# Second-layer and output weight splits in steps free of other work, with V's upper halves made by ScalarE

## The chip, the cores and the metric

The program runs on one core of a Trainium2 chip. A core has TensorE (PE in the profile, with its weight loads as PEld), VectorE (DVE), ScalarE (ACT), GpSimd (POOL) and SyncE (SP, which here only issues DMAs), and each engine works through its own queue in order. The metric is the device time of one execution in microseconds (us), as the median over the runs; less is better.

## The reference

The inputs are x (1 x 2048 x 640), wqkv (640 x 1920), wo (640 x 640), w1 (640 x 1536), b1, w2 (1536 x 640) and b2. A layer norm of x feeds two branches, and the result is the sum of x and both:

```python
xn = _layernorm(x)
return x + _A_ref(xn, wqkv, wo) + _B_ref(xn, w1, b1, w2, b2)
```

Branch A is attention with 32 heads of 20 columns each: q, k, v from `xn @ wqkv`, softmax of the scaled scores over all 2048 keys, times v, then `@ wo`. Branch B normalises `xn` once more, multiplies by w1, adds b1, applies the tanh form of gelu, multiplies by w2 and adds b2. Everything is float32 outside.

## The kernel before, in words

**Numbers in two halves.** A float32 operand of a product is split into an upper and a lower float16 half, and a product is three TensorE passes over them (upper-upper, upper-lower, lower-upper). Splitting a weight in place costs a scaling (`wtmp`), a cast to the upper half and a subtraction for the lower half. V is kept per block of 128 keys in `vfull`: blocks 0, 1, 4, 5, 8, 9, 12, 13 as an upper and a lower half (`SPLIT[kb]` is 1), the others whole.

**The head** (the first 186 us of the trace) takes x in four chunks of 512 rows: normalise, transpose (`pt`, then `xnt` in two halves: ScalarE casts the upper one, VectorE subtracts), and five pairs of q and k column blocks per chunk (`qk`), whose results leave PSUM through `qk_out` (ScalarE writes the upper half of `qkhl`, VectorE the lower half). `qk_sq` squares them (`sq`; in chunk 0 on ScalarE) for a bound on the scores. The order here is written out by hand, a string of letters for each pair, in which each letter is a step. V's columns of the first 8 heads are made here, and V of the last four key blocks whole.

**The loop** runs over 64 stretches: a pair of heads, one half of the query rows, one 512-column part of it. I call such a stretch an iteration. In it 16 units, one for each key block, each make scores (`s`, two matmuls), their exponentials on ScalarE (`p`, 128 x 1024), for the 8 split blocks a lower half on VectorE (`low`), and the product with V (`o`). ScalarE ends an iteration by moving `o` from PSUM (`ev`). Scores have three PSUM buffers, `p` has seven buffers and `low` four.

**What sets the order.** The table `PLAN` has seven rows for each iteration. `s` is a unit's scores, `lN` unit N's lower half, `v4` the V products of four units, `e` the evacuation, `t` and `r` each one tick, and `m` one slot for other TensorE work. The other TensorE work comes from one generator (`mlp`, then `projection`): for row chunk 0 of branch B the six first-layer products (`pu`), then V's remaining columns of the first twelve key blocks (`values`, product `pz`), then chunks 1 to 7 with the second layer (`py`), then the output projection (`z`). All of these use one PSUM buffer of one bank, `psM`, so that a product begins only when the one before has been read out. In each `m` slot so much of it is taken as a credit of some 1.9 us allows.

**Side work.** Everything that VectorE and ScalarE do for it (gelu, `values_out`, weight splits, stack loads) is a generator that takes one step for each tick. Those in the list `sides` take a step in every tick. Those in the list `patient` take one only if nothing else in that tick named a cost above zero. `values_out` runs its instructions when the last matmul of its `pz` is recorded and names a cost for the next tick. `second_split` splits w2 in 12 pieces, two steps each; `prep_late` loads wo into w1's place and splits it in 5 pieces, three steps each.

Of the kernel before, what the change touches and what calls it, by code (L numbers as in the profile page):

```python
# [13 lines left out]
AF = mybir.ActivationFunctionType  # L14
ALU = mybir.AluOpType
# [3 lines left out]
P = 128  # L19
# [16 lines left out]
RATE = (1.75, 1.95, 1.9)  # L36
PLAN = ('s s t l0 v4 e', 's s t l1 s r m r r l4', 's s l5 v4', 's s r t m', 's s s l8 r v4', 's l9 t l12 s l13 m', 's r s v4')
UNITS = (3, 3, 3, 3, 2, 2)
# [10 lines left out]
def mha_mlp_kernel(tc, x, wqkv, wo, w1, b1, w2, b2, out):  # L49
# [4 lines left out]
    with (  # L54
# [124 lines left out]
        with tc.tile_pool(name="pa", bufs=2) as pa, tc.tile_pool(name="pa1", bufs=1) as pa1, tc.manual_schedule():  # L179
# [181 lines left out]
            def qk_out(c, tt, ps):  # L361
                hl = stp.tile([P, 2, 2, 512], F16, tag="ks", name="qkhl")

                parts = ((0, 2),) if tt != 2 else ((0, 1), (1, 2))
                for i0, i1 in parts:
                    a = qks[:, (2 * tt + i0) // KD : (2 * tt + i0) // KD + 1]
                    nc.scalar.activation(hl[:, 0, i0:i1], ps[:, i0:i1], AF.Copy, scale=a)  # L367
                    nc.vector.scalar_tensor_tensor(hl[:, 1, i0:i1], ps[:, i0:i1], a, hl[:, 0, i0:i1],  # L368
                                                   ALU.mult, ALU.subtract)
                if c + tt > 0:  # L370
                    qk_sq(c, tt, hl)
                for s in range(2):
                    nc.sync.dma_start(
                        qkscr[s, 2 * tt * P : (2 * tt + 2) * P, c * 512 : (c + 1) * 512]
                        .rearrange("(i p) t -> p i t", p=P), hl[:, s])
                return hl
# [243 lines left out]
            for c in range(4):  # L620
                nxt = c + 1 if c < 3 else None
                for tt in range(5):
# [11 lines left out]
                    if c == 0:  # L634
# [5 lines left out]
                        elif tt == 1:  # L640
                            qk_sq(0, 0, hl)
                            pts = []
                    for step in (('', 'qvo', 'ao', 'bo', '4q!y@c#otyxttywz'), ('zos', 'qa6yqoPsbiqs', 'jkso', 'lcsV4o', 'sxoy'), ('ssoa6bzijP', 'yo', 'zs4ossc', 'klozV', 'uozs'), ('so', 'os6', 'oszs', 'ssosPsVfze4', 'o'))[c][tt]:
                        if step == "a":
# [29 lines left out]
                        elif step == "f":  # L674
                            factors_out()
                        elif step == "o":
                            qk_out(c, tt, ps)
                        elif step == "P":
# [25 lines left out]
        with ExitStack() as scope:  # L704
# [359 lines left out]
            def layer1(mc, f, spare=False):  # L1064
# [24 lines left out]
                if f == KF - 2:  # L1089
                    if 0 < mc < NMC - 2:  # L1090
                        load_chunk(mc + 2)
                    if mc + 1 == NMC:
                        sides.append(ahead())
                        sides.append(prep_late(wot, wov, wo.rearrange("(k p) n -> p k n", p=P), KD, 8))

# [8 lines left out]
            def layer2(mc, j, hf):  # L1104
# [5 lines left out]
                for f in range(KF):  # L1110
                    for a, b in PASS:
# [4 lines left out]
                        if n % 2 == 0:  # L1116
                            if n == 36:
                                begin(addup(ps, xbs[t0], t0, hf))
                            yield 0.272

            def second_split():

# [8 lines left out]
            def values_out(kb, ps):  # L1131

                pv_ = ps[:, : D - VC].rearrange("p (h d) -> p h d", d=DH)
                vs = (V16 if SPLIT[kb] else V32)[:, kb, VH:]
                nc.vector.tensor_scalar(vs[:, :, :DH], pv_, 2.0**-14, None, ALU.mult)  # L1135
                if SPLIT[kb]:
                    nc.vector.scalar_tensor_tensor(vs[:, :, VW : VW + DH], pv_, 2.0**-14, vs[:, :, :DH],  # L1137
                                                   ALU.mult, ALU.subtract)
                yield 1.2 if SPLIT[kb] else 0.6

            def values(hv, feats):

                step = (D - VC) / 2400
                for kb in range(NKB - 4):
                    c, j = divmod(kb, MC // P)
                    if kb == 8:
                        yield 1, 0.2
# [5 lines left out]
                        nc.vector.tensor_scalar(fo, pw["v"][0], 2.0**-22, pw["o"][0], ALU.mult, ALU.mult)  # L1153
                        sides.append(second_split())
                        yield 0.2
# [17 lines left out]
            def mlp():  # L1173
# [3 lines left out]
                for mc in range(NMC + 1):  # L1177
# [3 lines left out]
                    for i in range(6):  # L1181
# [7 lines left out]
                        if second and i % 3:  # L1189

                            yield 3 * KF // 2, 4.896
                            yield from second.pop(0)
# [275 lines left out]
```

## Time and profile before

| | |
|---|---|
| median of 3 runs | 1330.71 us (1330.6 to 1332.67) |
| the profiled execution's own time | 1334.18 us |
| its span, first to last instruction | 1332.3 us |
| PE busy in the span | 1317.0 us (99%) |
| ACT busy | 1111.4 us (83%) |
| DVE busy | 1072.6 us (81%) |
| granted TensorE clock | 0.996 of full speed |
| iterations of the loop, `ev` to `ev`, from 256.07 to 306.30 us | 16.97, 15.97 and 17.29 us |
| the next four | 18.51, 18.38, 18.41 and 17.16 us |

The busy time of PE is modelled, and a matmul that starts late behind a wait in its own group can still be counted as busy. So a full row of nines for PE does not say that it ran at its own pace; the length of like iterations does. A ScalarE or VectorE instruction's duration is from its start to its end, and two neighbours may overlap by a little.

### The profile page before, as it was taken

What the parts mean: (1) busy time and instruction counts of PE and PEld (TensorE: products, weight loads), DVE (VectorE), ACT (ScalarE), POOL (GpSimd) and SP (SyncE); (2) the same over time, 40 slices, a digit from 0 to 9 for tenths busy, and PEclk for the clock granted to TensorE, in tenths of its full rate; (3) what the DMA queues carried; (4) which work ended last, traced back from release to release, by engine and by line L of the source; (5) the groups of instructions that cost most, each with busy time, mean ns of one, the idle gap of its engine ahead of it and who ended that gap; (6) DMA issues with size and microseconds to landing.
All of it is one profiled execution on the core that took longest, in us unless ns stands there. A gap on an engine that the chain in (4) does not pass through costs nothing.

```text
span 1332.3 us, 29076 instructions
## 1 busy us (share of the span) xinstructions
PE 1317.0 (99%) x11636; PEld 606.0 (45%) x11636; DVE 1072.6 (81%) x1462; ACT 1111.4 (83%) x1294; POOL 36.3 (3%) x85
## 2 busy tenths in 40 slices
PE   9999999999999999999999999999999999999998
PEld 6455564333344444444444444444444444443466
DVE  6767659868999987889888888988889898988642
ACT  6744459898899999999999999999999999989900
POOL 2000000000000000000000000000000000000000
PEclk8999999999999999999999999999999999999999
DMA  8687631121223321142312033321124232253276
GB/s 286 216 268 211 197 122 35 39 68 42 62 79 102 93 54 32 47 117 69 98 51 64 20 88 117 81 56 58 49 58 118 91 83 73 71 157 98 88 218 188
DMA packets 108166, 135.28 MB, mean 102 GB/s; under 512 B 24308, under 2 KB 74376, under 8 KB 107900
## 3 DMA queue, kind: packets, MB, share of 16 engines
q1 hardware_dynamic: 104588, 125.99, 31.2%
q0 software_dynamic: 2816, 6.90, 2.7%
q8 instruction: 92, 1.51, 0.5%
q10 hardware_dynamic: 624, 0.51, 0.1%
q14 instruction: 46, 0.38, 0.1%
HBM read 86.64 MB, written 43.74 MB: 98 GB/s over the span
## 4 chain that ended last, share of the span: by engine, by line
PE 78%; DVE 13%; DMA 3%; ACT 3%; issue 2%; SPq 1%; ACTq 0%; DVEq 0%
PE o L816 25%; PE s L784 16%; PE pu L1077 10%; PE py L1112 10%; PE qkp L352 8%; DVE low L798 6%; PE z L1255 5%; ACT p L786 2%; PE pz L1161 2%; PE vp L425 1%; DVE w2t L1128 1%; DMA xb<-in_B_b_dram 1%; DVE u L1008 1%; DVE u L1010 1%; PE vp L446 1%
## 5 line engine op out<-in xcount | busy, mean ns | idle before, releaser
L786 ACT ACTIVATE p<-s 128x1024 f32<-128x1024 f32 x1024 | 968.4, 1053 | 68.2 <-PE s L784 66.6
L798 DVE TENSOR_TENSOR low<-p 128x1024 f16<-128x1024 f32 x512 | 605.5, 1219 | 65.8 <-ACT p L786 64.7
L816 PE MATMUL o<-p,vfull 128*32 128x512 bf16 (+1 forms) x4096 | 384.0, 493 | 0.0
L784 PE MATMUL s<-qs,ks 61*128 61x512 f16 x2048 | 302.9, 381 | 2.5 <-ACT p L786 1.7
L784 PEld LDWEIGHTS <-ks 61*128 61x128 f16 x2048 | 74.9, 94 | 231.4 <-issue 212.8
L1077 PE MATMUL pu<-xm,w1t 128*128 128x256 f16 x1440 | 171.4, 273 | 1.4 <-DVE vfull L1135 1.4
L1112 PE MATMUL py<-w2t,hT 128*128 128x320 f16 x1152 | 171.6, 300 | 1.2 <-DVE xb L1039 1.2
L1077 PEld LDWEIGHTS <-w1t 128*128 128x128 f16 x1440 | 134.3, 98 | 45.6 <-issue 31.1
L816 PEld LDWEIGHTS <-vfull 128*32 128x32 f16 x3072 | 61.3, 95 | 186.8 <-issue 186.2
L1112 PEld LDWEIGHTS <-hT 128*128 128x128 f16 x1152 | 105.6, 98 | 71.5 <-issue 34.2
L352 PE MATMUL qkp<-xnt,wv 128*128 128x512 f16 x600 | 132.2, 381 | 2.1 <-DVE xnt L322 1.6
L816 PE MATMUL o<-low,vfull 128*32 128x512 f16 x1024 | 102.7, 379 | 0.4 <-DVE low L798 0.3
L352 PEld LDWEIGHTS <-wv 128*128 128x128 f16 x600 | 58.7, 99 | 71.5 <-issue 3.3
L816 PEld LDWEIGHTS o<-p,vfull 128*32 128x32 f32 x2048 | 61.6, 108 | 58.3
L1255 PE MATMUL z<-w1t,ot 128*128 128x320 f16 x480 | 66.7, 299 | 0.0
L1008 DVE TENSOR_TENSOR u<-pu,r2f 128x512 f32<-128x512 f32 x48 | 33.1, 690 | 35.8 <-PE pu L1077 35.5
L1255 PEld LDWEIGHTS <-ot 128*128 128x128 f16 x480 | 46.3, 98 | 21.0 <-issue 3.3
L367 ACT ACTIVATE qkhl<-qkp,qks 128x1024 f16<-128x1024 f32 (+1 forms) x24 | 23.2, 966 | 38.1 <-PE qkp L352 22.8
L1212 DVE SCALAR_TENSOR_TENSOR acc<-z,sc,acc 128x320 f32<-128x320 f32 x32 | 17.6, 549 | 42.0 <-PE z L1255 39.7
L368 DVE SCALAR_TENSOR_TENSOR qkhl<-qkp,qks,qkhl 128x1024 f16<-128x1024 f32 (+1 forms) x24 | 26.5, 1105 | 25.2 <-ACT qkhl L367 25.2
L841 ACT ACTIVATE ev<-o 128x512 f32<-128x512 f32 x64 | 39.3, 614 | 3.7 <-PE o L816 3.5
L1161 PE MATMUL pz<-hv,xm 128*128 128x480 f16 x180 | 39.6, 367 | 0.8 <-DVE vfull L1137 0.8
(206 smaller groups left out, 713.7 us busy)
## 6 DMA issues: line engine op xcount, KB each, us to landing
qkscr<-qkhl SPq DMA_DIRECT2D x40, 256.0 KB
opart<-ev SPq DMA_DIRECT2D x124, 80.0 KB
ks<-qkscr SPq DMA_DIRECT2D x120, 80.0 KB
xm<-xscr SPq DMA_DIRECT2D x13, 640.0 KB
qs<-qkscr SPq DMA_DIRECT2D x192, 40.0 KB
oa<-opart SPq DMA_DIRECT2D x32, 240.0 KB
xt<-in_A_x_dram SPq DMA_DIRECT2D x16, 320.0 KB
xscr<-xnt SPq DMA_DIRECT2D x4, 1280.0 KB
```

What stands on the lines that cost most here:

```text
L352: nc.tensor.matmul(ps[:, i, :], wv[:, k, q, a, mm * P : (mm + 1) * P], xnts[c][:, k, b, :], start=(k + n == 0), stop=(k == KD - 1 and n == 2))
L368: nc.vector.scalar_tensor_tensor(hl[:, 1, i0:i1], ps[:, i0:i1], a, hl[:, 0, i0:i1], ALU.mult, ALU.subtract)
L784: nc.tensor.matmul(ps[:, a, :], ks[64 * a : 64 * a + 61, kb * P : (kb + 1) * P], qs[64 * a : 64 * a + 61, cc * 512 : (cc + 1) * 512], star ...
L786: nc.scalar.activation(pt, ps, AF.Exp, scale=QS)
L798: nc.vector.tensor_sub(low, pt, upper(pt))
L816: nc.tensor.matmul(pv.o[32 * q : 32 * q + 32, :], src[:, v0 - PAD * (1 - q % 2) :][:, :32], t, start=q not in pv.begun, stop=last, skip_gr ...
L841: nc.scalar.activation(evs[g, hf][:, cc], o, AF.Copy)
L1008: nc.vector.tensor_mul(u, ps, r2f[:, None, :].to_broadcast([P, 2, MC]))
L1077: nc.tensor.matmul(ps[:, i], w1v[:, k, (f + i) // 4, a, fo_ : fo_ + P], xnt[:, k, b, :], start=(n == 0), stop=(n == 3 * KD - 1))
L1112: nc.tensor.matmul(ps[:, :320], hTs[mc][:, f, a, j * P : (j + 1) * P], w2v[:, f, b, hf * 320 : (hf + 1) * 320], start=(n == 0), stop=(n == ...
L1161: nc.tensor.matmul(ps[:, : D - VC], feats[c][:, k, a, j * P : (j + 1) * P], hv[:, k, b, :], start=(n == 0), stop=(n == 3 * KD - 1))
L1255: nc.tensor.matmul(ps[:, :320], ot[:, k, a, j * P : (j + 1) * P], wov[:, k, b, h * 320 : (h + 1) * 320], start=(n == 0), stop=(n == 3 * KD ...
```

## The change

It has five parts.

1. `PLAN`: within three rows the letters `l0`, `l1`, `l5` and `e` change places with `v4`, `s` or each other, and one `t` becomes an `r`.
2. In the head, the square of chunk 0's fifth pair is taken out of `qk_out` and becomes a step `S` behind the three `t` steps, which write `xnt` of chunk 1.
3. `prep_late` goes into `patient`.
4. `second_split` is started at V's third block (`kb == 2`), and not at its ninth (`kb == 8`), and goes into `patient`. The second-layer factors and the scale of wo, with their small matmul `mxp`, come with it. Where a second-layer product is about to start, what is left of the split is done at once.
5. `values_out` writes the upper half (or the whole block) on ScalarE, and names smaller costs.

```diff
-PLAN = ('s s t l0 v4 e', 's s t l1 s r m r r l4', 's s l5 v4', 's s r t m', 's s s l8 r v4', 's l9 t l12 s l13 m', 's r s v4')
+PLAN = ('s s t v4 e l0', 's s t s l1 r m r r l4', 's s v4 l5', 's s r t m', 's s s l8 r v4', 's l9 r l12 s l13 m', 's r s v4')
...
-                if c + tt > 0:
+                if c + tt > 0 and (c, tt) != (0, 4):
                     qk_sq(c, tt, hl)
...
-'4q!y@c#otyxttywz'
+'4q!y@c#otyxttSywz'
...
+                        elif step == "S":
+                            qk_sq(0, 4, hl)
                         elif step == "o":
-                            qk_out(c, tt, ps)
+                            hl = qk_out(c, tt, ps)
...
-                        sides.append(prep_late(wot, wov, wo.rearrange("(k p) n -> p k n", p=P), KD, 8))
+                        patient.append(prep_late(wot, wov, wo.rearrange("(k p) n -> p k n", p=P), KD, 8))
...
-                nc.vector.tensor_scalar(vs[:, :, :DH], pv_, 2.0**-14, None, ALU.mult)
+                nc.scalar.activation(vs[:, :, :DH], pv_, AF.Copy, scale=2.0**-14)
                 if SPLIT[kb]:
...
-                yield 1.2 if SPLIT[kb] else 0.6
+                yield 0.8 if SPLIT[kb] else 0.1
...
-                    if kb == 8:
+                    if kb == 2:
                         yield 1, 0.2
...
-                        sides.append(second_split())
+                        late.append(second_split())
+                        patient.append(late[0])
...
                         if second and i % 3:
-
+                            if late and late[0] in patient:
+                                patient.remove(late[0])
+                                for _ in late[0]:
+                                    pass
+                            late.clear()
```

Part 1 moves nothing: with it alone, every engine's queue has the same rows in the same places, waits included, because the letters that change places stand for different engines with no tick between them.

Part 2 on ACT's queue, at chunk 0's end; `qkhl` is the upper half of q and k, `sq` its square, `xnt` the transposed rows of chunk 1, `wv` the split V weight. Before:

```order
L367 ACTIVATE qkhl<-qkp,qks 128x1024
L384 ACTIVATE sq<-qkhl 128x1024
L321 ACTIVATE xnt_605<-pt 128x2x512 x2
L321 ACTIVATE xnt_605<-pt_629 128x512
L476 ACTIVATE wv<-w1t,s_v 128x640 x5
```

After:

```order
L367 ACTIVATE qkhl<-qkp,qks 128x1024
L321 ACTIVATE xnt_605<-pt 128x2x512 x2
L321 ACTIVATE xnt_605<-pt_629 128x512
L384 ACTIVATE sq<-qkhl 128x1024
L476 ACTIVATE wv<-w1t,s_v 128x640 x5
```

The square now stands behind the three casts.

Parts 4 and 5 on DVE's queue, from V's first block on; `vfull<-pz` is a V block, `low` a lower half of the exponentials, `wtmp` and `w2t` the split of w2, `sc` and `lo_o` the small factors. Before:

```order
L1135 TENSOR_SCALAR vfull<-pz 128x24x20
L1137 SCALAR_TENSOR_TENSOR vfull<-pz,vfull 128x24x20
L798 TENSOR_TENSOR low<-p 128x1024 x6
L1135 TENSOR_SCALAR vfull<-pz 128x24x20
L1137 SCALAR_TENSOR_TENSOR vfull<-pz,vfull 128x24x20
L798 TENSOR_TENSOR low<-p 128x1024 x2
L1135 TENSOR_SCALAR vfull<-pz 128x24x20
L798 TENSOR_TENSOR low<-p 128x1024 x6
L1135 TENSOR_SCALAR vfull<-pz 128x24x20
L798 TENSOR_TENSOR low<-p 128x1024 x6
```

After, behind the same second block (its lower half, two `low`, then the nine small factors):

```order
L800 TENSOR_TENSOR low<-p 128x1024
L1129 TENSOR_SCALAR wtmp<-w2t,s_1643 128x640
L1130 CAST w2t<-wtmp 128x640
L800 TENSOR_TENSOR low<-p 128x1024
L1132 TENSOR_TENSOR w2t<-wtmp,w2t 128x640
L800 TENSOR_TENSOR low<-p 128x1024 x2
L1129 TENSOR_SCALAR wtmp<-w2t,s_1643 128x640
L1130 CAST w2t<-wtmp 128x640
L800 TENSOR_TENSOR low<-p 128x1024
L1132 TENSOR_TENSOR w2t<-wtmp,w2t 128x640
```

The twelve splits now begin in the 5th to the 8th iteration of the loop (two, four, four and two of them), between `low` instructions; before they began in the 8th to the 10th (two, five and five). The last of them stands well ahead of the first second-layer product, so that the loop that finishes them at once has nothing to do.

Part 5 on ACT's queue in the 5th iteration; `p` are the exponentials. Before:

```order
L1019 ACTIVATE w<-w 128x512
L786 ACTIVATE p<-s 128x1024 x9
L841 ACTIVATE ev<-o 128x512
L786 ACTIVATE p<-s 128x1024 x16
L841 ACTIVATE ev<-o 128x512
```

After:

```order
L1021 ACTIVATE w<-w 128x512
L1139 ACTIVATE vfull<-pz 128x24x20
L788 ACTIVATE p<-s 128x1024 x9
L843 ACTIVATE ev<-o 128x512
L788 ACTIVATE p<-s 128x1024 x3
L1139 ACTIVATE vfull<-pz 128x24x20
L788 ACTIVATE p<-s 128x1024 x9
L1139 ACTIVATE vfull<-pz 128x24x20
L788 ACTIVATE p<-s 128x1024 x4
L843 ACTIVATE ev<-o 128x512
```

One V block's copy stands ahead of `p` in each of the places where a `pz` ends, twelve in all.

On PE's queue `mxp` moves from the 8th iteration to the 5th, and six `pz` matmuls go from the 5th iteration to the 6th (29 become 23, and 24 become 30); nothing else moves there. The wo split at the end (part 3) has its first instructions where they were; two `low` that stood behind some of the later ones now stand ahead of them. DMA queues keep their order.

More of the change, by code (lines that the diff above doesn't have):

```diff
@@ L642, in mha_mlp_kernel @@
                             pts = []
-                    for step in (('', 'qvo', 'ao', 'bo', '4q!y@c#otyxttywz'), ('zos', 'qa6yqoPsbiqs', 'jkso', 'lcsV4o', 'sxoy'), ('ssoa6bzijP', 'yo', 'zs4ossc', 'klozV', 'uozs'), ('so', 'os6', 'oszs', 'ssosPsVfze4', 'o'))[c][tt]:
+                    for step in (('', 'qvo', 'ao', 'bo', '4q!y@c#otyxttSywz'), ('zos', 'qa6yqoPsbiqs', 'jkso', 'lcsV4o', 'sxoy'), ('ssoa6bzijP', 'yo', 'zs4ossc', 'klozV', 'uozs'), ('so', 'os6', 'oszs', 'ssosPsVfze4', 'o'))[c][tt]:
                         if step == "a":
@@ L1119, in layer2 @@
                             yield 0.272
+            late = []
             def second_split():
```

## Prediction

> **What bounds the kernel now.** I read the page first, then the length of the loop's iterations around the changed place (busy time by stretch, cut at the `ev` instructions), then the groups and waits inside them.
>
> ```profile
> span 1332.3 us, 29076 instructions
> PE 1317.0 (99%) x11636; PEld 606.0 (45%) x11636; DVE 1072.6 (81%) x1462; ACT 1111.4 (83%) x1294; POOL 36.3 (3%) x85
> ```
>
> TensorE is the bound of the whole, so a change elsewhere pays only where TensorE waits for it. The stretches, 5th to 11th iteration (length, then busy time of PE, PEld, DVE, ACT, POOL):
>
> ```profile
> 256.07:273.04 16.97, 16.97 (x143) 5.65 (x141) 11.23 (x12) 15.27 (x19) 0.00 (x0) 1.00 0.26 75
> 273.04:289.01 15.97, 15.97 (x138) 5.13 (x136) 11.41 (x12) 15.58 (x19) 0.00 (x0) 1.00 0.15 42
> 289.01:306.30 17.29, 17.29 (x144) 5.69 (x142) 11.26 (x12) 15.69 (x18) 0.00 (x0) 1.00 0.38 104
> 306.30:324.81 18.51, 17.73 (x146) 6.03 (x144) 15.72 (x27) 15.59 (x18) 0.00 (x0) 1.00 0.13 37
> 324.81:343.19 18.38, 17.43 (x144) 5.88 (x142) 18.07 (x25) 15.53 (x18) 0.00 (x0) 1.00 0.26 76
> 343.19:361.60 18.41, 16.56 (x144) 6.14 (x142) 18.10 (x24) 15.58 (x19) 0.00 (x0) 1.00 0.15 44
> 361.60:378.76 17.16, 16.83 (x159) 7.37 (x157) 16.71 (x24) 16.09 (x18) 0.00 (x0) 1.00 0.31 92
> ```
>
> In the first three TensorE never stops and VectorE is idle a third of the time. In the next four TensorE stops although it is given no more work, and in two of them VectorE is busy for 18.07 of 18.38 and 18.10 of 18.41 us: it is the bound there. How much is lost? The same stretches with the V products `pz` alone, then, in the last two rows, the first-layer products `pu` alone:
>
> ```profile
> 256.07:273.04 16.97, 6.40 (x29) 1.00 0.26 75
> 273.04:289.01 15.97, 5.38 (x24) 1.00 0.15 42
> 289.01:306.30 17.29, 6.60 (x30) 1.00 0.38 104
> 324.81:343.19 18.38, 6.58 (x30) 1.00 0.26 76
> 343.19:361.60 18.41, 3.38 (x15) 1.00 0.15 44
> ...
> 343.19:361.60 18.41, 1.80 (x15) 1.00 0.15 44
> 361.60:378.76 17.16, 5.43 (x45) 1.00 0.31 92
> ```
>
> Without its `pz`, an unhindered iteration is 16.97 - 6.40 = 10.57, 15.97 - 5.38 = 10.59 and 17.29 - 6.60 = 10.69 us: 10.62 for the attention part. So TensorE needs 17.22 us with 30 `pz`, 10.62 + 3.38 + 1.80 = 15.80 in the 10th, and 10.62 + 5.43 = 16.05 in the 11th. The 8th holds 30 `pz` too and the small `mxp` (0.4 us, row below), 17.62. Lost are 18.51 - 17.62 = 0.89, 18.38 - 17.22 = 1.16, 18.41 - 15.80 = 2.61 and 17.16 - 16.05 = 1.11, in all 5.77 us. What VectorE does there (groups from 306.3 to 361.6 us: count | busy, mean ns), and what TensorE waited for (306.3 to 378.8 us: total, times, longest):
>
> ```profile
> L798 DVE TENSOR_TENSOR low<-p 128x1024 f16<-128x1024 f32 x24 | 28.7, 1219 | 1.6 <-ACT p L786 1.4
> L1128 DVE TENSOR_TENSOR w2t<-wtmp,w2t 128x640 f16<-128x640 f32 x11 | 9.1, 823 | 0.2
> L1125 DVE TENSOR_SCALAR wtmp<-w2t,s 128x640 f32<-128x640 f32 x12 | 6.6, 549 | 0.1
> L1126 DVE CAST w2t<-wtmp 128x640 f16<-128x640 f32 x11 | 5.4, 494 | 0.4
> L1137 DVE SCALAR_TENSOR_TENSOR vfull<-pz,vfull 128x480 f16<-128x480 f32 x2 | 1.3, 660 | 0.1
> L1135 DVE TENSOR_SCALAR vfull<-pz 128x480 f16<-128x480 f32 x2 | 1.3, 652 | 0.0
> L118 PE MATMUL mxp<-acco,wones 128*128 128x5 f32 x2 | 0.4, 264 | 0.0
> ...
> PE pu L1077 <- DVE vfull L1135: 1.4, 1, 1.4
> PE pz L1161 <- DVE vfull L1137: 0.8, 1, 0.8
> ```
>
> A split piece is 0.82 + 0.55 + 0.49 = 1.87 us, a `low` 28.7 / 24 = 1.20. The two named waits are for the one PSUM buffer, which VectorE reads out too late.
>
> **The change, part by part.** `PLAN`: no queue's order changes, waits included, so nothing.
>
> *V's upper halves to ScalarE.* VectorE loses twelve instructions of 0.65 us, 7.8 us in all. ScalarE gains twelve of 128 x 480. It does none of that size from PSUM before; the nearest rows are the same function on V's other parts:
>
> ```profile
> L614 ACT ACTIVATE vfull<-vp 128x160 f16<-128x160 f32 x6 | 1.8, 295 | 2.9 <-DVE vfull L616 2.9
> L435 ACT ACTIVATE vfull<-vp 128x640 f16<-128x640 f32 x2 | 1.4, 707 | 6.3 <-PE vp L425 6.3
> ```
>
> 480 lies between, at 295 + 320/480 x 412 = 570 ns; the ends are 295 and 707, so twelve cost 3.5 to 8.5 us, and I take 6.8. Where do they fall? ScalarE's queue is in order, so the copy waits for `pz` and the exponentials queue behind it. But just after a `pz` ScalarE has nothing to do:
>
> ```profile
> 310.57 1.94 ACT L786 ACTIVATE p<-s 128x1024 f32<-128x1024 f32 x2 [0.93 <-PE s L784]
> 320.82 1.94 ACT L786 ACTIVATE p<-s 128x1024 f32<-128x1024 f32 x2 [1.60 <-PE s L784]
> ```
>
> It had been idle for 0.93 and 1.60 us and waited for the next scores, so a copy of 0.57 fits. By iteration: two copies on 15.58 give 16.72 us of ScalarE, under the 17.22 that TensorE needs with 30 `pz`; covered. In the 10th, one copy gives 16.15 against 15.80: 0.35 us lost. In the 5th, which now has 23 `pz` and `mxp`, TensorE needs 10.62 + 23 x 0.22 + 0.4 = 16.08 and ScalarE 16.72: 0.64 lost; and the slot that `mxp` leaves empty cost 0.89 in the 8th, so I take 0.9 (0.64 to 1.5, were both to add).
>
> By the Trainium skill, Perfetto Trace Analysis, section Identifying the Most-Contended Engine, the engine of vector and scalar work with the highest occupancy is the one to optimise first. By the first three stretches that is ScalarE, 46.5 of 50.2 us against VectorE's 33.9, and the change loads it: the rule speaks against this part and would have those iterations wait for ScalarE (priced among the rivals). The trace of the next three says the opposite.
>
> *The split of w2 earlier and patient.* The 9th and 10th iteration lose it wholly: VectorE has 10.0 us of work or less there (8 x 1.20 and a lower half), so 1.16 and 2.61 go, but for the 0.35 above. The 6th and 7th get four pieces each: 8 x 1.20 + 4 x 1.87 + 0.66 = 17.7 us against 17.22. VectorE falls behind by 0.5 in each, 1.0 in all. Is there room? The `low` pair that ends latest against its use, in an unhindered iteration:
>
> ```profile
> 301.12 2.36 DVE L798 TENSOR_TENSOR low<-p 128x1024 f16<-128x1024 f32 x2 [1.39 <-ACT p L786]
> ...
> 305.86 0.39 PE L816 MATMUL o<-low,vfull 128*32 128x512 f16 x4
> ```
>
> Ready at 303.48, used at 305.86: 2.38 us of lag cost nothing, and neighbours of these two iterations leave VectorE 2 us to recover. I take 0. The 8th, with two pieces and no `mxp`: 0.
>
> *The 11th iteration* holds three gelus beside `low`: VectorE's 16.71 us, and one small `r2f` scaling more, 17.1 in all against 16.05:
>
> ```profile
> L1031 DVE TENSOR_SCALAR r2f<-r2f,sc 128x256 f32<-128x256 f32 x3 | 1.0, 349 | 0.0
> ```
>
> It lost 1.11 because VectorE came into it late. Now it comes in rested, and 1.0 fits into 2.38: I take 0.2 for the PSUM buffer being read late once.
>
> So the stage still loses 0.9 + 0.35 + 0.2 = 1.45 of 5.77: gain 4.3 us.
>
> *The square in the head.* Timeline at chunk 0's end:
>
> ```profile
> 51.96 1.06 ACT L384 ACTIVATE sq<-qkhl 128x1024 bf16<-128x1024 f16 x1
> 51.96 1.28 DVE L368 SCALAR_TENSOR_TENSOR qkhl<-qkp,qks,qkhl 128x1024 f16<-128x1024 f32 x1 [0.64 <-ACT qkhl L367]
> 52.92 2.41 ACT L321 ACTIVATE xnt<-pt 128x1024 f16<-128x1024 f32 x3
> 53.96 2.95 DVE L322 TENSOR_TENSOR xnt<-pt,xnt 128x1024 f16<-128x1024 f32 x3 [0.72 <-ACT xnt L321]
> 55.24 10.95 PE L352 MATMUL qkp<-xnt,wv 128*128 128x512 f16 x50 [1.56 <-DVE xnt L322]
> ```
>
> TensorE is idle for 1.56 us until the first `xnt` is done. Without the square ahead, ScalarE's cast ends about 0.9 us earlier and VectorE, free at 53.24, starts at once and not at 53.96: 0.72 us. Behind the casts the square takes time in which ScalarE waits anyway. Later in the head the chain of waits goes over one DMA of a weight, which may take the lead back:
>
> ```profile
> 82.28 5.40 DMA w1t<-in_B_w_dram
> ```
>
> The ends are 0 and 0.72, and I take 0.5, since that DMA is issued behind work that moves up too.
>
> *The wo split, patient.* Its first instructions keep their place, and it stays ahead of the first output product. Near it TensorE waits once, for an addition that waits for its bias by DMA:
>
> ```profile
> 1195.69 0.55 DVE L1039 SCALAR_TENSOR_TENSOR xb<-py,sc,xb 128x320 f32<-128x320 f32 x1 [2.67 <-DMA xb<-in_B_b_dram]
> ...
> 1196.30 2.88 PE L1112 MATMUL py<-w2t,hT 128*128 128x320 f16 x20 [1.23 <-DVE xb L1039]
> ```
>
> Nothing of the change touches that DMA. I take 0, between -0.3 and +0.3 for two `low` that trade places with pieces.
>
> Sum: 4.3 + 0.5 = 4.8 us. The profiled execution, 1334.18 us of its own time (1.9 around the span), would be 1329.4; the median of the runs lies 3.5 lower than it, and 1330.7 - 4.8 gives 1325.9 us.
>
> **The rivals.** *VectorE is only late elsewhere.* If the lag buys nothing, the 6th and 7th iteration run at 17.7 us over 98.3% (the 18.07 of 18.38 above), 18.0: 0.8 lost in each; the 11th keeps its 1.0, the 5th 0.9, the 10th 0.35. That is 3.85 of 5.77: the gain is 1.9, with the head 2.4, and 1328.3 us; without the head 1328.8. For it speaks that the pieces come four to an iteration; against it the 2.38 us.
>
> *ScalarE becomes the bound: slower.* Where exponentials wait behind each copy, all 6.8 us go on the path; and in the six split blocks VectorE's lower half (0.66) cannot start until ScalarE is through, which keeps the PSUM buffer: 6 x 0.66 = 4.0. 10.8 - 4.8 = 6.0 more: 1336.7. It decides from (4.8 + 2.7) / 12 = 0.63 us for each block on. The idle 0.93 and 1.60 speak against it; that ScalarE has only 50.2 - 46.5 = 3.7 us free in three iterations speaks for it.
>
> *The change does not do what it says.* The splits could stay undone until the second layer and then come in one burst of 22 us; the order excludes it, since all twelve stand before the 11th iteration.
>
> **How the numbers follow.** A measurement of this kernel can tell some 0.2%, 2.7 us, from no change. The forecast (two thirds or more of the stage's loss gone, 1324 to 1327.5) has 0.66; the first rival, 1327.5 to 1330.5, 0.22, of which a good quarter is still faster by over 0.2%; ScalarE as the bound 0.08; something else, with no change to be told, 0.04. So faster 0.72, same 0.20, slower 0.08. The range goes from 1323.9 (5.77 + 0.72, with 0.3 from the end) to 1329.6, which leaves out the slow rival and the worst of the first.
>
> **What would show it.** Right: the 9th and 10th iteration at about 17.2 and 16.2 us, VectorE at 55% to 60% in them; no wait of `pu` or `pz` for `vfull` over 0.5 us; the copies at 0.55 to 0.6 us; the first `qkp` of chunk 1 some 0.7 us earlier, and the loop starting 0.5 to 0.7 earlier. Wrong: the 6th and 7th at 18 us with VectorE full, or ScalarE without a gap and TensorE waiting for `p` or for ScalarE's `vfull` in many iterations.

## The result, and the profile after

The kernel after takes 1328.21 us as the median of 17 runs (1326.66 to 1330.88), the kernel before, measured beside it, 1331.06 us as the median of 17 (1329.85 to 1334.87). The ratio is 0.9977, with a 95% interval from 0.9969 to 0.9984: 2.1 to 4.1 us faster, where 4.8 were forecast. All ratios here and below, with their intervals, come from all the runs and not from the two medians, so they can differ from the medians' ratio by up to 0.0007. The profiled execution of after took 1328.16 us.

The page of after, its span and the busy time of the engines:

```profile
span 1326.3 us, 29078 instructions
PE 1314.0 (99%) x11636; PEld 604.2 (46%) x11636; DVE 1065.3 (80%) x1450; ACT 1116.3 (84%) x1306; POOL 36.1 (3%) x85
```

VectorE lost twelve instructions and ScalarE gained twelve; 1065.3 against 1072.6 and 1116.3 against 1111.4 us are as the change says. The span is 6.0 us shorter, more than the medians differ. Half of that has nothing to do with the change, as the head will show.

The stretches of the loop, 5th to 11th iteration, with the columns of before (length, then busy time of PE, PEld, DVE, ACT, POOL, granted clock, DMA share, GB/s):

```profile
253.00:270.66 17.66, 16.40 (x139) 5.61 (x137) 13.75 (x24) 16.34 (x20) 0.00 (x0) 1.00 0.25 72
270.66:287.83 17.17, 17.17 (x144) 5.74 (x142) 16.69 (x22) 16.35 (x21) 0.00 (x0) 1.00 0.14 39
287.83:305.13 17.30, 17.30 (x144) 5.75 (x142) 16.00 (x22) 16.61 (x21) 0.00 (x0) 1.00 0.38 104
305.13:322.44 17.31, 17.31 (x144) 5.82 (x142) 14.84 (x17) 16.30 (x20) 0.00 (x0) 1.00 0.13 39
322.44:339.93 17.49, 17.36 (x144) 5.82 (x142) 10.04 (x10) 16.45 (x20) 0.00 (x0) 1.00 0.31 80
339.93:356.22 16.29, 15.96 (x144) 5.77 (x142) 9.50 (x9) 15.87 (x19) 0.00 (x0) 1.00 0.17 49
356.22:372.25 16.03, 16.03 (x159) 7.35 (x157) 15.06 (x23) 15.85 (x19) 0.00 (x0) 1.00 0.35 100
```

The 8th to the 11th came down from 18.51, 18.38, 18.41 and 17.16 us to 17.31, 17.49, 16.29 and 16.03. The 5th went up, from 16.97 to 17.66, although it has six V products fewer. From the 4th to the 12th iteration, nine in all, 157.55 us became 154.15: 3.4 us, and this is the gain.

The groups of the copies that moved (count | busy, mean ns of one | idle time ahead, releaser), and all that TensorE waited for from 235 to 390 us (total, times, longest):

```profile
L1139 ACT ACTIVATE vfull<-pz 128x480 f16<-128x480 f32 x6 | 3.5, 588 | 2.1 <-PE pz L1166 2.1
L1139 ACT ACTIVATE vfull<-pz 128x480 f32<-128x480 f32 x6 | 3.5, 586 | 2.9 <-PE pz L1166 2.9
```

```profile
PE s L786 <- ACT p L788: 1.8, 5, 0.5
```

A copy takes 0.587 us (0.570 was worked out). The two waits for `vfull`, 1.4 and 0.8 us before, are gone, and what is left is a wait of scores for exponentials. Most of it, 1.3 of the 1.8 us, is in the 5th iteration. There the timeline of after reads (start, us, engine, line, what it does, idle time just before it and its releaser):

```profile
256.21 0.62 ACT L1139 ACTIVATE vfull<-pz 128x480 f16<-128x480 f32 x1
256.66 8.41 ACT L788 ACTIVATE p<-s 128x1024 f32<-128x1024 f32 x9
...
258.11 0.39 PE L118 MATMUL mxp<-acco,wones 128*128 128x5 f32 x2
258.70 0.39 PE L786 MATMUL s<-qs,ks 61*128 61x512 f16 x2 [0.21 <-ACT p L788]
...
259.62 0.39 PE L786 MATMUL s<-qs,ks 61*128 61x512 f16 x2 [0.53 <-ACT p L788]
...
260.53 0.39 PE L786 MATMUL s<-qs,ks 61*128 61x512 f16 x2 [0.52 <-ACT p L788]
```

In the slot that should hold V products TensorE does only `mxp` (0.39 us), and runs ahead into scores whose buffers ScalarE has not yet read. ScalarE does nine exponentials without a gap, 0.93 us each, and the copy of V's block stands ahead of them.

### The profile page after: what moved, and what is told of

Same layout as the page of the kernel before. It is cut to its first block, busy times and chain, and to the rows that moved or that the text cites. A ratio compares the mean times of both kernels' runs of the same rounds, so it can differ in the third digit from the quotient of the medians.

```text
span 1326.3 us, 29078 instructions
## 1 busy us (share of the span) xinstructions
PE 1314.0 (99%) x11636; PEld 604.2 (46%) x11636; DVE 1065.3 (80%) x1450; ACT 1116.3 (84%) x1306; POOL 36.1 (3%) x85
## 4 chain that ended last, share of the span: by engine, by line
PE 72%; DVE 15%; ACT 5%; DMA 4%; issue 2%; SPq 1%; ACTq 0%; DVEq 0%; POOLq 0%
PE o L818 23%; PE s L786 15%; PE pu L1079 10%; PE py L1114 8%; DVE low L800 6%; PE qkp L352 6%; PE z L1264 5%; PE pz L1166 3%; ACT p L788 2%; PE vp L425 1%; DMA xb<-in_B_b_dram 1%; DVE w L1014 1%; DVE u L1012 1%; DVE u L1010 1%; DVE w L1016 1%
## 5 line engine op out<-in xcount | busy, mean ns | idle before, releaser
L1104 POOL DMA_DIRECT2D xb<-in_B_b_dram x16 | 13.7, 857 | 953.7 <-DMA xb<-in_A_x_dram 352.4
```

## The experiments

The stage's nine iterations, 4th to 12th, are compared by their sum, which repeats well: 157.48, 157.45 and 157.41 us in the traces of three kernels that leave this stage as it was (the square alone, the table alone, the wo split alone), against 157.55 before.

**The parts one by one.** The square in the head alone, on the kernel before:

```diff
-                if c + tt > 0:
+                if c + tt > 0 and (c, tt) != (0, 4):
                     qk_sq(c, tt, hl)
...
-'4q!y@c#otyxttywz'
+'4q!y@c#otyxttSywz'
...
+                        elif step == "S":
+                            qk_sq(0, 4, hl)
...
```

> The kernel before with the square alone moved behind the casts of chunk 1. My theory: the first product of chunk 1 starts 0.7 us sooner against the end of the transposes (its wait falls from 1.56 to about 0.85 us), and 0.5 us of that reaches the end: ratio 0.9996, 1330.2 to 1330.9 us where the kernel before has 1331.1. The loop's stretch of nine iterations stays at 157.5 us. Rival: the wait at 93 us for work behind a weight's DMA takes the lead back and the ratio is 1.0000.

It measured 1331.31 us against 1331.29, ratio 0.9999 (0.999 to 1.0008): nothing. The counterpart, the kernel after with the square left where it was:

```diff
-                if c + tt > 0 and (c, tt) != (0, 4):
+                if c + tt > 0:
                     qk_sq(c, tt, hl)
...
-'4q!y@c#otyxttSywz'
+'4q!y@c#otyxttywz'
...
```

> The changed kernel with the square back ahead of the casts of chunk 1. My theory: the first scores of the loop come 0.5 us later than in the changed kernel where the clock at the start was the same, with the nine iterations at 154.1 us; ratio to the kernel before 0.9980 to 0.9985. Rival (the lead is given back in the head): no difference from the changed kernel, 0.9977.

It measured 1327.94 us, ratio 0.9977 (0.9968 to 0.9986), the same as the kernel after. Together with the run before it, the square moves no more than this comparison can tell, about 0.1%.

`PLAN` alone, on the kernel before:

```diff
-PLAN = ('s s t l0 v4 e', 's s t l1 s r m r r l4', 's s l5 v4', 's s r t m', 's s s l8 r v4', 's l9 t l12 s l13 m', 's r s v4')
+PLAN = ('s s t v4 e l0', 's s t s l1 r m r r l4', 's s v4 l5', 's s r t m', 's s s l8 r v4', 's l9 r l12 s l13 m', 's r s v4')
```

> The kernel before with the new table of steps alone, whose queues hold the same rows in the same places. My theory: ratio 1.0000, and what it differs from that by is what the measurement of this kernel can tell (0.001 or less); nine iterations 157.5 us. Rival (the table acts by some route that the queues do not show): a difference of over 0.3 us in the nine iterations.

1331.38 us against 1330.84, ratio 1.0005 (0.9996 to 1.0014). Since the queues are the same, this is also what two measurements of one program can differ by.

The trace of this kernel, whose head is that of before, says why the square gains nothing. The timeline at chunk 0's end, with the square still ahead of the casts:

```profile
49.37 1.28 DVE L368 SCALAR_TENSOR_TENSOR qkhl<-qkp,qks,qkhl 128x1024 f16<-128x1024 f32 x1
50.66 2.95 DVE L322 TENSOR_TENSOR xnt<-pt,xnt 128x1024 f16<-128x1024 f32 x3
...
51.94 2.32 PE L352 MATMUL qkp<-xnt,wv 128*128 128x512 f16 x10 [0.84 <-DVE xnt L322]
```

and the same place of the kernel after:

```profile
50.59 2.94 DVE L322 TENSOR_TENSOR xnt<-pt,xnt 128x1024 f16<-128x1024 f32 x3
...
51.85 2.32 PE L352 MATMUL qkp<-xnt,wv 128*128 128x512 f16 x10 [0.75 <-DVE xnt L322]
```

VectorE comes to `xnt` straight from the lower half of `qkhl`, at 50.65 us, and does not wait for ScalarE's cast. The move saves 0.84 - 0.75 = 0.09 us, and none of it is seen at the loop: the 4th iteration starts at 235.86 us in the kernel after and at 235.60 in the one with the table alone. The prediction read 1.56 and 0.72 us in the same place, but in an execution that had run part of the head on half a clock. The profile of before, by stretches, and then what ScalarE waited for ahead of the upper half of `qkhl` at chunk 0's end:

```profile
12.20:19.00 6.80, 6.55 (x29) 5.28 (x28) 4.10 (x12) 3.94 (x10) 0.00 (x0) 0.50 0.72 207
...
50.81 1.11 ACT L367 ACTIVATE qkhl<-qkp,qks 128x1024 f16<-128x1024 f32 x1 [1.94 <-PE qkp L352]
```

The granted clock was 0.50 for 6.8 us. The products came late: ScalarE waited 1.94 us for them, and its casts came later than VectorE, which in the traces at full clock did not have to wait for them. The 4th iteration of that trace starts at 238.94 us, and at 235.86 (after), 235.93 (the square alone) and 235.60 (the table alone) in traces whose head had the full clock: about 3 us of the difference of the spans are this. The Trainium skill, TensorE: Matmul & The Clock Gate, section Terms, puts the penalty at about the throttled time times one minus the granted share; as an estimate that is 6.8 x 0.5 = 3.4 us here, and the traces, at 3.0 to 3.3, agree roughly.

The wo split in `patient` alone, on the kernel before:

```diff
-                        sides.append(prep_late(wot, wov, wo.rearrange("(k p) n -> p k n", p=P), KD, 8))
+                        patient.append(prep_late(wot, wov, wo.rearrange("(k p) n -> p k n", p=P), KD, 8))
```

> The kernel before with only the split of wo made patient. My theory: no difference to be told, within 0.3 us (ratio 0.9998 to 1.0002); the 60th iteration, at 18.6 us, keeps its wait for the bias's DMA. Rival: VectorE is late there, and two lower halves ahead of the pieces save 0.5 us or more of it.

1331.16 us against 1331.29, ratio 1.0001 (0.9992 to 1.001), as costed.

V's upper halves on ScalarE alone:

```diff
-                nc.vector.tensor_scalar(vs[:, :, :DH], pv_, 2.0**-14, None, ALU.mult)
+                nc.scalar.activation(vs[:, :, :DH], pv_, AF.Copy, scale=2.0**-14)
...
-                yield 1.2 if SPLIT[kb] else 0.6
+                yield 0.8 if SPLIT[kb] else 0.1
```

> The kernel before with V's upper halves alone on ScalarE; the split of w2 stays at V's ninth block. My theory: VectorE loses 1.3 us in the 8th and 9th and 0.65 us in the 10th iteration, and the copies are covered on ScalarE but for 0.6 us in the iteration with the small matmul: the nine iterations go from 157.5 to about 155.8 us (155.0 to 156.5), ratio 0.9985 to 0.9995. Rival (ScalarE's queue is the bound, copies stand on the path): 12 x 0.57 = 6.8 us more, less 2.5: slower, 160 us or more, ratio over 1.002.

1329.61 us against 1331.29, ratio 0.9994 (0.9981 to 1.0006), so the timings alone do not show a gain; in the trace the nine iterations take 155.93 us, 1.6 less. Its 6th, 9th and 10th:

```profile
270.56:286.87 16.31, 16.11 (x138) 5.22 (x136) 10.19 (x10) 16.27 (x20) 0.00 (x0) 1.00 0.14 41
...
322.68:340.32 17.64, 17.40 (x144) 5.86 (x142) 17.33 (x24) 16.44 (x20) 0.00 (x0) 1.00 0.27 79
340.32:357.62 17.30, 16.53 (x144) 6.07 (x142) 17.04 (x22) 15.96 (x19) 0.00 (x0) 1.00 0.16 46
```

The 9th and 10th go from 18.38 and 18.41 to 17.64 and 17.30: with 0.65 us less per block VectorE still is the bound there, and less so. The 6th, with 24 V products, goes from 15.97 to 16.31, and ScalarE is busy in 16.27 of it: there it is the bound, for 0.34 us. So both engines can be, each in its own iterations. The rule of the highest occupancy from the Trainium skill, Perfetto Trace Analysis, section Identifying the Most-Contended Engine, points to ScalarE when it is taken over the nine iterations of before (141.47 us busy against VectorE's 135.42), and yet loading ScalarE shortened the stage. Taken over the 9th and 10th alone (15.53 and 15.58 against 18.07 and 18.10) it points to VectorE, and there the runs agree with it.

The early split alone:

```diff
-                    if kb == 8:
+                    if kb == 2:
...
-                        sides.append(second_split())
+                        late.append(second_split())
+                        patient.append(late[0])
...
+                            if late and late[0] in patient:
+                                patient.remove(late[0])
+                                for _ in late[0]:
+                                    pass
+                            late.clear()
```

> The kernel before with the split of w2 alone started at V's third block and made patient; V's upper halves stay on VectorE. My theory (VectorE's load by iteration decides): the 6th and 7th iteration then ask 8 x 1.20 + 4 x 1.87 + 0.66 + 2 x 0.65 = 19.0 us of VectorE against TensorE's 17.2, so they take 18 to 18.7 us, while the 9th and 10th fall to 17.2 and 15.8; the nine iterations lose 1 to 2.5 us of 157.5 (155.0 to 156.5), ratio 0.9985 to 0.9995. Rival (moving the splits is all that counts, VectorE's lag absorbs the rest): as much as with both parts, 154.2 us, ratio 0.998.

1329.15 us against 1331.29, ratio 0.9985 (0.9976 to 0.9994); the nine iterations 154.78 us, 2.8 less, most of the whole and a little better than the 155.0 to 156.5 expected: VectorE was busy for 16.40 and 17.41 us in the 6th and 7th, and not for 19.0. The 5th, 8th and 10th:

```profile
255.01:272.22 17.21, 16.32 (x139) 5.45 (x137) 14.96 (x26) 15.41 (x18) 0.00 (x0) 1.00 0.26 74
...
307.02:325.30 18.28, 17.72 (x144) 6.00 (x142) 16.99 (x22) 15.59 (x18) 0.00 (x0) 1.00 0.12 37
...
342.77:359.06 16.29, 15.96 (x144) 5.75 (x143) 9.99 (x10) 15.48 (x18) 0.00 (x0) 1.00 0.17 49
```

Three things are in these rows. The 5th loses 17.21 - 16.08 = 1.13 us without any copy on ScalarE. The 8th runs at 18.28, and 17.31 after: without the copies VectorE falls behind so far in the 6th and 7th that the 8th pays for it (TensorE waits there 0.4 us for `vfull` and 0.2 for `low`, both from VectorE), and this is what the copies on ScalarE are worth beside the early split: 0.6 us of the stage in the traces (154.78 against 154.15), too little for the timings to tell. And the 10th has 16.29 us with no copy in ScalarE's queue, exactly as after, so its remaining loss is not the copy's. Alone the two parts gain 1.6 and 2.8 us, together 3.4: they take off the same load in the 9th and 10th.

**Is it early or patient?** The kernel after, with the split started as early but stepping in every tick:

```diff
-                        patient.append(late[0])
+                        sides.append(late[0])
```

> The kernel after, but the split of w2, started at V's third block as there, steps in every tick and is not patient: five or six of its twelve pieces fall into each of the 6th and the 7th iteration, where the kernel after has four. Theory: VectorE then has 8 x 1.20 + 5 x 1.87 + 0.66 = 19.6 us in an iteration for which TensorE needs 17.2, falls behind by 2.4 in each, and only the first 2.4 us of lag are free, so the 6th and 7th together take 36 to 37 us instead of 34.47, the nine iterations 155.2 to 157, and the ratio comes to 0.998 to 0.9995. Rival: that the split is early is all that counts, since the 8th iteration is free to recover in; then the nine iterations stay at 154.2 and the ratio at 0.9975.

1328.94 us against 1331.11, ratio 0.999 (0.9981 to 0.9999). The 6th and 7th:

```profile
270.75:287.92 17.17, 17.17 (x144) 5.75 (x142) 16.89 (x23) 16.35 (x21) 0.00 (x0) 1.00 0.13 39
287.92:306.11 18.19, 17.75 (x144) 6.01 (x142) 17.92 (x24) 16.76 (x21) 0.00 (x0) 1.00 0.38 98
```

The 6th loses nothing, the 7th 0.9 us with VectorE busy in 17.92 of 18.19; the nine iterations take 154.84, under the 155.2 to 157 expected. The direction is the theory's, the size about half of it: VectorE had 16.89 and 17.92 us of work in the two iterations and not 19.6 in each. What the lag does is seen in the tightest pair of lower halves of the 7th, first in the kernel after, then without patience:

```profile
301.75 2.36 DVE L800 TENSOR_TENSOR low<-p 128x1024 f16<-128x1024 f32 x2
304.69 0.39 PE L818 MATMUL o<-low,vfull 128*32 128x512 f16 x4
```

```profile
303.26 2.36 DVE L800 TENSOR_TENSOR low<-p 128x1024 f16<-128x1024 f32 x2
305.67 0.40 PE L818 MATMUL o<-low,vfull 128*32 128x512 f16 x3 [0.44 <-DVE low L800]
```

In the kernel after it is ready at 304.11 us, 0.58 ahead of its use, where the prediction had read 2.38 in an unhindered iteration: the lag used up 1.8 us of that and cost nothing. Without patience it is used up whole, and TensorE waits. So the early start is most of this part's worth, and patience some 0.7 us in the traces (154.84 against 154.15); the intervals of the two timings overlap.

**What the 5th iteration lost.** It lost 17.66 - 16.08 = 1.58 us; 0.9 was forecast. Three runs split it. First, two of the twelve copies back on VectorE:

```diff
-                nc.scalar.activation(vs[:, :, :DH], pv_, AF.Copy, scale=2.0**-14)
+                if kb in (1, 2):
+                    nc.vector.tensor_scalar(vs[:, :, :DH], pv_, 2.0**-14, None, ALU.mult)
+                else:
+                    nc.scalar.activation(vs[:, :, :DH], pv_, AF.Copy, scale=2.0**-14)
```

> The kernel after, but V's second and third block (the two whose products run in the 5th iteration) get their upper halves from VectorE again. Theory: the 5th iteration of the kernel after lost 1.58 us (17.66 against a need of 16.08) in two parts, the slot that mxp leaves empty, and two copies on a ScalarE that has no room there. With VectorE's copies only the first part is left, as in the run with the early split alone, where that iteration lost 1.13: it comes to 17.2 us, the others stay, the nine iterations come to 153.7 us instead of 154.15, and the ratio to the kernel before is 0.997 to 0.9975. Rival: the copies cost nothing there and the empty slot costs it all; then the 5th stays at 17.6 to 17.7.

1327.63 us against 1331.2, ratio 0.9975 (0.9965 to 0.9984). The 5th iteration, and in it ScalarE and TensorE:

```profile
253.92:271.13 17.21, 16.32 (x139) 5.45 (x137) 14.95 (x26) 15.40 (x18) 0.00 (x0) 1.00 0.26 74
```

```profile
254.42 11.11 ACT L788 ACTIVATE p<-s 128x1024 f32<-128x1024 f32 x12
```

```profile
258.99 0.39 PE L118 MATMUL mxp<-acco,wones 128*128 128x5 f32 x2
259.31 0.39 PE L786 MATMUL s<-qs,ks 61*128 61x512 f16 x2
260.07 0.39 PE L786 MATMUL s<-qs,ks 61*128 61x512 f16 x2 [0.37 <-ACT p L788]
260.99 0.39 PE L786 MATMUL s<-qs,ks 61*128 61x512 f16 x2 [0.52 <-ACT p L788]
```

17.21 us, as with the early split alone: the empty slot costs 1.13 and the copies 0.45. The first wait is gone and the second shorter. Even without a copy ScalarE does twelve exponentials in a row, 0.93 us each, so work put in front of them goes onto the path. Each of the two lengths comes back in a second trace: 17.21 with the early split alone, 17.66 in the run that is not patient. The nine iterations came to 153.50 us (153.7 expected).

Second, the slot put elsewhere, by starting split and `mxp` at V's fifth block:

```diff
-                    if kb == 2:
+                    if kb == 4:
```

> The kernel after, with the split and mxp started at V's fifth block and not at its third, so that mxp's slot lies in the 6th iteration (24 V products) and the twelve pieces in the 6th to the 9th (two, four, four, two). Theory: the empty slot costs 1.1 to 1.6 us wherever it lies, so the 5th comes down to 17.0 and the 6th goes up by as much, the 9th rises by 0 to 0.3 for its two pieces, and the nine iterations come to 154.1, give or take 0.5: ratio 0.997 to 0.998. Rival: the slot is cheaper where fewer V products stand; then the nine iterations come to 153.2 or less.

1328.78 us against 1331.2, ratio 0.9983 (0.9974 to 0.9992); the nine iterations 153.86. The 5th came down to 16.99, and the 6th and 9th read:

```profile
270.24:287.98 17.74, 16.59 (x140) 5.71 (x138) 14.06 (x24) 16.38 (x21) 0.00 (x0) 1.00 0.13 38
...
322.59:340.07 17.48, 17.35 (x144) 5.79 (x142) 14.34 (x17) 16.44 (x21) 0.00 (x0) 1.00 0.29 80
```

The 6th needs 10.62 + 24 x 0.22 + 0.4 = 16.30 and loses 1.44, with two copies in it, where the 5th lost 1.58 with two copies: the slot costs about the same in both places. The 9th took two pieces of the split at no cost.

Third, no slot of its own: `mxp` in one of the buffers of the scores, in a slot together with V products.

```diff
-                if tag in "ko":
+                if tag == "k":
...
-                        yield 1, 0.2
...
-                        yield 0.2
```

> The changed kernel, but the small matmul for wo's scale has no slot of its own: it goes ahead of V's third block in that block's slot, and writes a score buffer in place of the shared PSUM buffer. My theory (the slot it left empty, with the copies on top, is the 1.6 us lost in the 5th iteration): the 5th iteration takes 17.4 us with 29 V products and no score waits there; the 6th, now with 24, is ScalarE's at 16.3 (as in the run with the copies alone); nine iterations 152.9 us (152.6 to 153.4) against the changed kernel's 154.15, ratio to the kernel before 0.9965 to 0.9975. Rival (VectorE's nine small factors and the lower halves behind them cost it): 154 us as before.

1333.27 us against 1330.84, ratio 1.0015 (1.0006 to 1.0024): slower than before. The place itself did improve, 17.88 + 16.32 = 34.20 us for the 5th and 6th against 34.83 after, with the same V products, though not to the 17.4 expected of the 5th: `mxp` waits there 0.6 us for the exponentials whose buffer it takes. The nine iterations came to 154.03 us and not to 152.9. And the rest of the loop, from the 12th evacuation on, and the waits of scores in it:

```profile
390.05:1269.62 879.57, 876.48 (x8203) 382.72 (x8200) 746.89 (x902) 819.96 (x923) 14.51 (x17) 1.00 0.28 78
```

```profile
PE s L786 <- ACT p L788: 2.1, 7, 0.4
```

against the kernel after:

```profile
390.01:1264.64 874.63, 872.58 (x8203) 381.18 (x8200) 746.03 (x901) 820.28 (x924) 14.23 (x17) 1.00 0.28 78
```

```profile
PE s L786 <- ACT p L788: 0.4, 1, 0.4
```

4.9 us more for the same work. The same edit on the kernel with the early split alone:

> The kernel before with the early split alone (upper halves on VectorE) and the small matmul sharing the slot. My theory: the 5th iteration loses nothing (17.4 us), the 6th has 24 V products and needs 16.0 but VectorE 19.0, so its lag carries into the 7th and 8th: about 17, 18.2 and 18.3 us; nine iterations 154.5 us (153.8 to 155.2), ratio 0.998. Rival (the copies were never needed): 153 us, as with them on ScalarE.

1333.38 us against 1330.84, ratio 1.0018 (1.0009 to 1.0028), with the nine iterations at 154.49 us, as expected, and 878.35 us in the rest of the loop: the same again. One slot fewer moves every later product by one slot against the attention units. Whether that is the cause, or the sharing of the scores' buffer, the next run tells apart. It keeps `mxp` there and leaves one slot empty behind V's last block, so that all later products stand where they did:

```diff
+                yield 1, 0.2
+                yield 0.2
```

> The kernel after with mxp put into a slot together with V products (no slot of its own), as in the run before that lost 5 us in the rest of the loop, and one slot left empty behind V's last block, so that from there on every product stands in the same slot as in the kernel after. Theory: the 5 us came from nothing but the place of all later products against the attention units, so the rest of the loop (11th iteration's start to the 63rd) comes back from 879.6 to 874 to 875 us, and the loss of the empty slot moves from the 5th to the 10th iteration or shrinks there; in all 0.996 to 0.998 of the kernel before. Rival: sharing the buffer of the scores does the harm itself; then the rest of the loop stays at 878 to 880 us and the ratio at 1.0015.

1327.69 us against 1331.2, ratio 0.9976 (0.9967 to 0.9985). Its 5th and 10th iteration, and the rest of the loop:

```profile
253.21:271.07 17.86, 17.24 (x145) 6.08 (x143) 13.34 (x24) 16.10 (x20) 0.00 (x0) 1.00 0.25 71
...
339.53:355.14 15.61, 14.49 (x129) 4.51 (x127) 9.36 (x9) 15.60 (x19) 0.00 (x0) 1.00 0.18 51
```

```profile
390.38:1263.79 873.41, 872.08 (x8203) 381.25 (x8200) 745.90 (x901) 820.12 (x924) 14.25 (x17) 1.00 0.28 78
```

The 5 us are gone, with `mxp` still in the scores' buffer: it was the place of the products and not the buffer. The empty slot's loss is now in the 10th, which has 15 V products, needs 10.62 + 3.38 = 14.00 us and takes 15.61, with ScalarE busy in 15.60 of it. So the slot that `mxp` leaves empty buys something: it sets the place of all that follows. Where the loss lies, the two traces with `mxp` in the scores' buffer show: in the 13th to the 40th iteration, while from there to the end the one without the slot is 0.4 us the shorter. These iterations without the slot and with it, each with its products of the lower halves (count | busy, mean ns of one | idle time ahead, releaser):

```profile
390.05:866.54 476.49, 473.76 (x4434) 208.27 (x4432) 404.81 (x481) 443.57 (x502) 6.83 (x8) 1.00 0.27 73
...
L818 PE MATMUL o<-low,vfull 128*32 128x512 f16 x448 | 46.6, 379 | 0.4 <-DVE low L800 0.2
```

```profile
390.38:860.29 469.91, 469.49 (x4434) 206.82 (x4432) 404.18 (x480) 443.49 (x501) 6.78 (x8) 1.00 0.27 74
...
L818 PE MATMUL o<-low,vfull 128*32 128x512 f16 x448 | 44.3, 378 | 0.0
```

Of the 6.6 us only 2.3 are idle time of TensorE, nearly all of it waits of scores for exponentials (2.1 us). The other 4.3 are counted as busy for the same 4434 matmuls, 2.3 of them in the products of the lower halves. That these wait for VectorE inside their groups fits, but is not shown; nor which of the later products stands badly.

Among the variants the kernel with two copies back (1327.63 us), the one with an empty slot behind V's last block (1327.69) and the kernel after (1328.21) have overlapping intervals; none is shown to beat the kernel after.

## Why the prediction was right, and where it was off

The sign and the place were right, the size too large: 4.8 us forecast, 2.85 measured between the medians (2.1 to 4.1). The time lies in the whole range, but above the band of the forecast itself (1324 to 1327.5) and in that of the first rival; the stage gave back 3.4 of its 5.77 us, less than the two thirds that the forecast asked for. In the traces it is 3.4 in the stage and nothing that reaches the loop from the head. By its steps:

- *`PLAN`: 0.* Held (1.0005, with 0.9996 to 1.0014).
- *The copies: twelve at 570 ns, covered.* 587 ns, and covered in the 6th to the 9th iteration, where TensorE with 30 V products runs at 17.17 to 17.49 us against its 17.22. Not covered in the 5th.
- *The 5th iteration: 0.9 (0.64 to 1.5).* This term failed most: 1.58. The working took the larger of two causes, an empty slot (0.89) and a ScalarE loaded beyond TensorE's need (0.64, from a load of 16.72 us; the 5th's own row, 15.27, would have given 16.41, and 16.34 was measured). They add: 1.13 and 0.45. ScalarE's load over the iteration, 16.34 of 17.66 us, does not show why; around the empty slot it does nine to twelve exponentials without a gap. The gaps of 0.93 and 1.60 us that the prediction showed stand behind a full slot of V products, and the empty slot has none.
- *The 6th and 7th: 0, by 2.38 us of lag.* Held, in 17.17 and 17.30 us with four pieces each, and the lag is seen in the rows above. VectorE's load was smaller than the 17.7 us worked out, 16.69 and 16.00: the sum took whole durations, though neighbours overlap by some 0.1 us, and a part of the work ends in the 8th. The run that is not patient shows where the lag ends: about five pieces and a block, VectorE at 17.92 us, cost 0.9.
- *The 9th: 0; the 10th: 0.35; the 11th: 0.2.* 17.49 - 17.22 = 0.27, 16.29 - 15.80 = 0.49 and 16.03 - 16.05, nothing. The reason given for the 10th, a copy on ScalarE, was wrong: without the copy it is 16.29 as well. TensorE waits there 0.33 us for an exponential, behind a slot of five V products. In the 11th VectorE had 15.06 us of work and not 17.1: the 16.71 of before held what was left of the split.
- *Stage: 4.3.* 3.4. Of the 0.9 missing 0.7 is the 5th; the rest is the 9th and 10th, less the 11th.
- *The square: 0.5 (0 to 0.72).* 0.09 at its place, and nothing at the loop. The row it came from, 1.56 us of idle TensorE, was read in the one trace at hand, and that stretch of it followed 6.8 us at half clock. That the profiled execution lay 3.5 us over the median was noted, and taken off the time alone, not off the durations. The granted clock by stretches would have told it.
- *The wo split: 0.* Held (1.0001).

The other signs the prediction named came out: the 9th and 10th near 17.2 and 16.2 us, VectorE at 57% and 58% in them, no wait for `vfull`, copies of 0.59 us. The first product of chunk 1 and the loop did come 3.4 and 3.1 us earlier than in the trace of before, but because of the clock, as the run with the table alone shows, which starts its 4th iteration at 235.60 us.

The rivals: that VectorE is only late elsewhere gave 1328.3 us, and 1328.21 was measured, nearer than the forecast's 1325.9, yet by chance and not by its mechanism. It asked for 18.0 us in the 6th and 7th and a loss of 1.0 in the 11th; they took 17.17, 17.30 and 16.03. That ScalarE becomes the bound fell as a slower outcome: the copies alone shorten the stage by 1.6 us. What is true in it is small and has its place, 0.34 us where an iteration has 24 V products and 0.45 beside the empty slot.

Of the 2.3 us between 1325.9 and 1328.21, 0.9 is the stage, 0.5 the head, and 0.35 that the kernel before itself came to 1331.06 and not 1330.7 over more runs. The other 0.55 is inside the interval of the measurement.

## What to carry to other kernels

An engine's room for a new instruction is read where the instruction lands, not from its load over the whole iteration: nine exponentials without a gap leave no room, though the iteration shows one. A slot left empty lets TensorE run into work that another engine has not finished (1.1 us here), and a slot taken away moves everything behind it (4.9 us here); both are counted before the queue is made shorter. Before a wait of a single trace is priced, the granted clock around it is looked up.

## What was not expected

**Where the products stand is worth more than the change.** Taking one slot of 0.4 us of work away cost 4.9 us over the next 52 iterations, and putting an empty one back 5 iterations later regained 6.2 (879.57 against 873.41).

**Half-clock stretches differ from run to run.** The trace of before has one early in the head; that of the kernel after without the square's move has one within the 5th iteration:

```profile
261.70:265.10 3.40, 3.40 (x19) 0.52 (x11) 3.37 (x5) 2.52 (x3) 0.00 (x0) 0.50 0.01 3
```

That iteration took 19.24 us and not 17.66: 1.58 more, about half of the 3.40 us. The row counts TensorE as busy for the whole stretch. TensorE had waited at the empty slot just before it; but it waits as long in the kernel after, at full clock, so what brings such a stretch is not shown. A comparison of single iterations is only as good as the clock in them.

**One DMA near the end moves the span by 1 us from run to run.** The bias add of the 60th iteration waits for its DMA, in after and in the kernel with the early split alone (waits from 1180 to 1200 us):

```profile
DVE xb L1041 <- DMA xb<-in_B_b_dram: 2.4, 1, 2.4
```

```profile
DVE xb L1039 <- DMA xb<-in_B_b_dram: 1.5, 1, 1.5
```

No variant touches it, and it was 2.7 us in the trace of before. TensorE waited 1.2 us behind it before and 0.9 after; in the second trace it did not wait. It is one reason that the rest of the loop differs by up to 1.8 us (872.87 to 874.63) between traces of the same products in the same slots; a second buffer for that bias was not tried.
